# The state product in strips of 32 columns directly behind the output product, and the output product in turns over four column groups

## The chip, the cores and the metric

The kernel runs on one NeuronCore of a Trainium2 chip. The metric is the device time of one execution in microseconds (us), the median of several runs. One further execution was profiled; its trace is what the rows below come from. Engines are named as in the profile: PE (matrix products), PEld (the loading of PE's stationary operand), DVE (vector engine), ACT (scalar engine), POOL, SP (which here issues the DMA transfers).

## The reference

A gated linear recurrence over 768 time steps, for 4 batches and 8 heads of size 48, followed by two pairs of dense layers on the 3072 tokens:

```python
mag = np.sqrt(a_re * a_re + a_im * a_im)
scale = np.minimum(mag, 0.999) / (mag + 1e-06)
...
for t in range(S):
    new_re = ar * S_re - ai * S_im
    new_im = ar * S_im + ai * S_re
    S_re, S_im = (new_re + outer(k[t], v[t]), new_im)
    y[:, :, t] = np.einsum('bhd,bhde->bhe', q[:, :, t], S_re)
x = y as (3072, 384)
h = x @ w_in;   x = (h - tanh(h)) @ w_out       # d_ff 2048
h = x @ w_in2;  r = max(h, 0);  out = (r * r) @ w_out2
```

## The kernel before

**Attention in chunks.** The 768 steps are cut into 6 chunks of 128. One chunk of one batch is a *unit*; there are 24, numbered 4 x chunk + batch. Inside a chunk the recurrence is turned into products: keys and queries are scaled by cumulated decay and phase (`kn`, `qn`; the phase gives each head 96 rows, real and imaginary parts in turns), transposed on PE (`pk`, `pq`, copied by ACT to `kqT`), multiplied to scores (`sc`), masked by DVE (`wm`), and two products follow:

- the *output product* `px` (function `a12`): the masked scores with the values `v` (called intra below), and from chunk 1 on the queries with the state of that batch (inter). Heads of 48 columns are cut into 12 groups G of 32 output columns, so that each product is a 32-column strip which goes to the partitions of column group G % 4 of a PSUM tile, in the k-slice G // 4. A group that holds the seam of two heads has two parts.
- the *state product* `pU` (function `a13`): `kn` with `v` for each of 8 heads, 48 moving columns; DVE then updates the state from it (`a13v`, two instructions). It isn't needed in the last chunk. From chunk 2 on `kn` lies *packed*: heads 0 to 5 as 96 adjacent columns, heads 6 and 7 as three strips of 32 each.

All these are float32, and each such product of the program shows as two MATMUL records in the trace (32 products of a `px` are 64 records). The products of the dense layers are in a split form with single records.

**What runs beside it.** The dense layers are cut into *blocks*: one block is a slice of 128 of d_ff for a group of 512 tokens, 9 products into `h` (L228), ACT and DVE work on `h` (for the first layer pair `t` by tanh, `t<-h,t`, the cast `gh`, the rest `gl`), and, two blocks later, 9 products into `acc` (L260 to L262). A token group is one chunk of all four batches, so chunk c's attention is computed while the blocks of chunk c - 1 run. Chunk 0 runs before all blocks in an order written out by hand (START, up to about 56 us); chunk 1 beside the first 17 blocks, in which DVE also converts the weights (`cv`, `wh`, `wl`) just ahead of their use.

**Order.** A unit has 16 or so steps; its list gives (step, kind, function), units of a chunk start 4 steps apart, and from chunk 2 on each block runs one step of every live unit. Kind "p" stands in front of the block's `h` products, "e", "v", "p2", "v2" behind them. The transposes of `kn` and `qn` are step 13, the scores 14, the output product 15. The state product is in step 15 for chunks 0 to 2 and in step 16, one block later, from chunk 3 on:

```python
(14, "p2" if packed else "p", a11), ..., (15, "p", a12), (15, "v", a12v),
(NST - (c < 3), "p", a13), (NST - (c < 3), "v", a13v),      # NST = 16
```

A scheduler behind the kernel takes this order and its dependences and writes each engine's final row of instructions; each engine works its own row in order. Unit n + 1 makes `kn` and `qn` (DVE, `a9`, behind two ACT sines into `fg`) in the block after unit n's step 15, and its transposes come one block later. The load of `ri` for a later unit is issued by SP in the same stretch, and ACT squares it on arrival (`ab<-ri`, L384).

Of the kernel before, what the change touches and what calls it, by code (L numbers as in the profile page):

```python
# [43 lines left out]
def kernel(  # L44
# [9 lines left out]
    nc = tc.nc  # L54
# [3 lines left out]
    P = 128  # L58
# [4 lines left out]
    KD = DM // P  # L63
    NU = B * NC
    D2 = 2 * D
    HH = H // 2
# [258 lines left out]
    def strip(z, h, i):  # L325
        o = DP * h + 32 * i - (DP - D) * (h % 2)
        return z.rearrange("p h x -> p (h x)")[:, o:o + 32]
# [5 lines left out]
    def unit(n):  # L333
        c, b = divmod(n, B)
        alt = n in (1, 3)
        early_unit = 1 <= n <= 3
        def bank(name):
            if n >= 2:
                return ps_a.tile([P, TG], F32, tag="a", name=name)
            spin[0] = (spin[0] + 1) % 8  # L340
            pool, tag = [(ps_a, "a"), (ps_c, "c"), (ps_h, "h")][(0, 1, 2, 0, 1, 2, 0, 1)[spin[0]]]
            return pool.tile([P, TG], F32, tag=tag, name=name)
# [3 lines left out]
        V = {}  # L346
# [21 lines left out]
        packed = c >= 2  # L368
# [173 lines left out]
        def head(name, h):  # L542
            i, j = slot(h)
            return T(name, i)[:D2, j, :]
# [50 lines left out]
        def a12():  # L595
            px = bank("px")
            vv = V["v"]
            parts = {}
            for G in range(3 * HH):
                r, g = divmod(G, 3)  # L600
                parts[G] = [((2 * r, 0),), ((2 * r, 1), (2 * r + 1, 0)), ((2 * r + 1, 1),)][g]
            for kk in range(KD):
                Gs = range(4 * kk, 4 * kk + 4)
                seq = []
                for inter in ((True, False) if c > 0 else (False,)):
                    for i in range(2):
                        seq += [(G, inter) + parts[G][i] for G in Gs if i < len(parts[G])]
                for j, (G, inter, h, sl) in enumerate(seq):
                    i, jj = divmod(h, HH)
                    if inter:  # L610
                        z, mv = stt[b][:D2], head("qT", h)
                    else:
                        z, mv = vv, V["wm", i][:, jj, :]
                    q0 = 32 * (G % 4)
                    nc.tensor.matmul(  # L615
                        px[q0:q0 + 32, kk * P:(kk + 1) * P],
                        strip(z, h, sl), mv,
                        start=all(e[0] != G for e in seq[:j]),
                        stop=all(e[0] != G for e in seq[j + 1:]),
                    )  # L620
            V["px"] = px

# [15 lines left out]
        def a13():  # L638
            if c + 1 == NC:
                return  # L640
            pU = bank("pU")
            for h in range(H):
                vh = V["v"][:, h, :D]
                hs = slice(h * D, (h + 1) * D)
                if packed and h >= 6:
                    for j in range(3):
                        o = (3 * (h - 6) + j) * P + D2
                        nc.tensor.matmul(
                            pU[32 * j:32 * j + 32, hs], V["kn"][:, o:o + 32], vh,
                            start=True, stop=True,  # L650
                        )
                else:
                    o = h * (P if packed else D2)
                    nc.tensor.matmul(  # L654
                        pU[:D2, hs], V["kn"][:, o:o + D2], vh, start=True, stop=True
                    )
            V["pU"] = pU

# [14 lines left out]
        if c == 0:  # L673
            return dict(
                ld=a0, sq=a1, ln=a2, ph=a3, pc=a6l, ee=a7x, at=a4, pu=a6, rd=a7, lq=l2, lv=l3,
                qe=a8x, sn=a8, er=a7r, kn=lambda: a9((("kn", "k"),)), qn=lambda: a9((("qn", "q"),)),
                t0=t0, e0=t0v, t1=t1_, e1=t1v, s0=lambda: a11((0,)), s1=lambda: a11((1,)),
                m0=lambda: a11v((0,)), m1=lambda: a11v((1,)),
                px=a12, x=a12v, pU=a13, st=a13v, ff=fill,
            )  # L680
# [4 lines left out]
            (12, "e", a8), (12, "e", l3), (12, "e", a9),  # L685
            (13, "p", t0), (13, "v", t0v), (13, "p2", t1_), (13, "v2", t1v),
            (14, "p2" if packed else "p", a11), (14, "v2" if packed else "v", a11v), (15, "p", a12), (15, "v", a12v),
            (NST - (c < 3), "p", a13), (NST - (c < 3), "v", a13v),
        ]

    NST = 16
    plan = {}
    for n in range(B, NU):
        c, b = divmod(n, B)
        s0 = (c - 1) * NM + 3 + 4 * b - (NST - 1)
        for i, kind, f in unit(n):
            plan.setdefault((s0 + int(i), kind), []).append(f)
# [190 lines left out]
    hs, gs = {}, {}  # L888
# [84 lines left out]


    first = {f"{n}{k}": f for n in range(B) for k, f in unit(n).items()}
    first.update(C=clear_pads, W=conv_ahead, J=conv_tick, B=lambda: block_step(0))
    for k in START.split():
# [97 lines left out]
```

## Time and profile before

| | |
|---|---|
| median of 3 runs | 1009.43 us (1008.85 to 1010.75) |
| the profiled execution's own time | 1011.25 us |
| its span, first to last instruction | 1009.3 us |
| PE busy | 983.8 us, 97% of the span |
| ACT busy | 640.0 us, 63% |
| DVE busy | 540.8 us, 54% |

The span is what the trace covers, and the time is the span and some 2 us around it. The shares are means over very unlike stages: attention runs up to about 536 us, the second layer pair alone fills the rest.

### The profile page before, as it was taken

The page shows a single profiled execution, that of the slowest core. Times are in us where ns is not written, and L with a number is a line of the kernel's source. Part 1 is how long each engine was busy: PE and PEld are TensorE (multiplying, and loading weights), DVE is VectorE, ACT ScalarE, POOL GpSimd, SP SyncE. Part 2 cuts the span into 40 slices and gives each one's busy share as a digit, 9 for nine tenths or more (in the row PEclk, how much of TensorE's full clock was granted, in tenths as well). Part 3 has the DMA queues.
Part 4 walks back from the last instruction along what each step waited for, and adds up shares of the span by engine and source line. Part 5 has one row for each costly group of instructions (what it writes and reads, how often), then busy time and mean ns, then how long its engine had stood idle before and what let it go on. Part 6 is the DMA issues. An engine that isn't in the chain of part 4 may idle for free.

```text
span 1009.3 us, 15932 instructions
## 1 busy us (share of the span) xinstructions
PE 983.8 (97%) x6112; PEld 814.5 (81%) x6112; DVE 540.8 (54%) x900; ACT 640.0 (63%) x1132; POOL 17.1 (2%) x37
## 2 busy tenths in 40 slices
PE   3999999999999999999999999999999999999997
PEld 1877788888788888888887888888888888888886
DVE  6899998988866566666534553122232322322111
ACT  8679898766777776667633445456565665555542
POOL 1000000000000000000000000000000000000000
PEclk9999999999999999999999999999999999999999
DMA  7444554665652222112105332025263444330000
GB/s 260 122 126 141 169 147 128 192 192 195 218 144 50 52 82 60 52 51 81 40 23 194 104 95 94 1 79 172 94 207 104 143 140 142 109 110 32 32 0 34
DMA packets 61546, 111.35 MB, mean 110 GB/s; under 512 B 23685, under 2 KB 33177, under 8 KB 61465
## 3 DMA queue, kind: packets, MB, share of 16 engines
q1 hardware_dynamic: 61320, 110.15, 34.9%
q8 instruction: 49, 0.80, 0.3%
q14 instruction: 33, 0.26, 0.1%
q10 hardware_dynamic: 144, 0.13, 0.0%
HBM read 91.29 MB, written 15.76 MB: 106 GB/s over the span
## 4 chain that ended last, share of the span: by engine, by line
PE 80%; DVE 7%; ACT 6%; DMA 5%; issue 1%; SPq 0%; POOL 0%; ACTq 0%; DVEq 0%
PE h L228 33%; PE acc L260 11%; PE acc L262 11%; PE acc L261 11%; PE px L615 4%; PE sc L578 3%; PE pU L654 2%; DMA st<-in_w_dram 2%; ACT L118 2%; DMA ri<-in_ri_dram 2%; PE pq L553 1%; PE pk L553 1%; ACT ab L125 1%; DVE cv L161 1%; DVE gl L249 1%
## 5 line engine op out<-in xcount | busy, mean ns | idle before, releaser
L249 DVE TENSOR_TENSOR gl<-t,gh 128x512 fp32r<-128x512 f32 (+1 forms) x193 | 132.4, 686 | 251.9 <-ACT gh L248 251.6
L228 PE MATMUL h<-xh,wh 128*128 128x512 f32 (+1 forms) x579 | 230.8, 399 | 0.3 <-DVE t L244 0.3
L260 PE MATMUL acc<-gh,wh 128*128 128x512 f32 (+1 forms) x579 | 227.7, 394 | 1.5 <-ACT x2t L271 1.4
L228 PE MATMUL h<-xl,wh 128*128 128x512 f32 (+1 forms) x579 | 225.8, 390 | 0.0
L228 PE MATMUL h<-xh,wl 128*128 128x512 f32 (+1 forms) x579 | 225.4, 389 | 0.0
L262 PE MATMUL acc<-gh,wl 128*128 128x512 f32 (+1 forms) x579 | 225.3, 389 | 0.0
L261 PE MATMUL acc<-gl,wh 128*128 128x512 f32 (+1 forms) x579 | 225.2, 389 | 0.0
L248 ACT CAST gh<-t 128x512 fp32r<-128x512 f32 (+1 forms) x193 | 118.9, 617 | 71.5 <-PE acc L262 63.5
L246 ACT ACTIVATE t<-h 128x512 f32<-128x512 f32 x96 | 57.4, 598 | 126.2 <-PE h L228 126.2
L228 PEld LDWEIGHTS h<-xh,wh 128*128 128x128 f32 x579 | 108.7, 188 | 26.2 <-issue 2.6
L260 PEld LDWEIGHTS acc<-gh,wh 128*128 128x128 f32 x579 | 108.8, 188 | 23.4 <-ACT x2t L271 2.6
L228 PEld LDWEIGHTS h<-xh,wl 128*128 128x128 f32 x579 | 108.7, 188 | 23.2
L262 PEld LDWEIGHTS acc<-gh,wl 128*128 128x128 f32 x579 | 108.7, 188 | 22.9
L228 PEld LDWEIGHTS h<-xl,wh 128*128 128x128 f32 x579 | 108.8, 188 | 21.0 <-DVE xl L634 0.2
L261 PEld LDWEIGHTS acc<-gl,wh 128*128 128x128 f32 x579 | 108.8, 188 | 20.8
L125 ACT ACTIVATE t<-h 128x512 f32<-128x512 f32 (+1 forms) x97 | 57.2, 590 | 66.9 <-PE h L228 65.3
L118 ACT ACT_TABLE_LOAD x66 | 84.7, 1283 | 2.0 <-PEq L1057 0.8
L244 DVE TENSOR_TENSOR t<-h,t 128x512 f32<-128x512 f32 (+1 forms) x97 | 65.9, 680 | 35.9 <-ACT t L125 35.7
L247 ACT ACTIVATE t<-t 128x512 f32<-128x512 f32 x96 | 60.3, 628 | 1.6
L192 DVE TENSOR_TENSOR wmin<-wmin,cz 128x768 bf16<-128x768 bf16 x32 | 17.8, 557 | 57.4 <-ACT cz L189 57.4
L578 PEld LDWEIGHTS sc<-kqT 96*128 96x128 f32 x352 | 42.7, 192 | 2.0 <-ACT kqT L562 0.2
L578 PE MATMUL sc<-kqT 96*128 96x128 f32 x352 | 43.5, 276 | 0.0
(128 smaller groups left out, 1078.1 us busy)
## 6 DMA issues: line engine op xcount, KB each, us to landing
st<-in_w_dram SPq DMA_DIRECT2D x32, 768.0 KB, 4.6
sr<-in_w_dram SPq DMA_DIRECT2D x32, 768.0 KB, 4.7
ri<-in_ri_dram SPq DMA_DIRECT2D x24, 384.0 KB, 4.1
qk<-in_qk_dram SPq DMA_DIRECT2D x24, 384.0 KB, 5.6
w2d<-cv SPq DMA_DIRECT2D x16, 384.0 KB, 2.6
jw<-w2d SPq DMA_DIRECT2D x16, 384.0 KB, 3.0
vz<-in_v_dram SPq DMA_DIRECT2D x21, 256.0 KB, 3.1
x2d<-x2t SPq DMA_DIRECT2D x18, 256.0 KB, 2.4
```

The lines of the kernel that those rows point to most:

```text
L118: load = nc.scalar.preload_act_table_set(name).ins
L125: r = nc.scalar.activation(*a, **kw)
L228: nc.tensor.matmul(h, w_[:, kk * P:(kk + 1) * P], x_[:, kk, cs], start=(i == 0), stop=(i == n - 1),)
L244: nc.vector.tensor_tensor(t, h, t, op=ALU.subtract)
L246: last["act"] = nc.scalar.activation(t, h, AF.Relu).ins
L247: nc.scalar.activation(t, t, AF.Square)
L248: nc.scalar.copy(gh, t)
L249: nc.vector.tensor_tensor(gl, t, gh.bitcast(F32), op=ALU.subtract)
L260: nc.tensor.matmul(o, wh[:, sl], gh, start=first, stop=False)
L261: nc.tensor.matmul(o, wh[:, sl], gl, start=False, stop=False)
L262: nc.tensor.matmul(o, wl[:, sl], gh, start=False, stop=end)
L578: nc.tensor.matmul(sc[:, j, :], head("kT", i * HH + j), head("qT", i * HH + j), start=True, stop=True,)
```

## The change

Three edits. (1) In `a12` the 32 products of a unit (16 in chunk 0) are no longer issued slice by slice; each of the four column groups gets its own list (groups g, g + 4, g + 8, each with its inter and intra parts), and the lists are issued in turns, one product of each column group after the other. (2) In `a13` every head, not only the two packed apart, is cut into three strips of 32 stationary columns: 24 products in place of 8 (chunks 0 and 1) or 12 (chunks 2 to 4). (3) From chunk 3 on the state product and the state update move from step 16 to step 15, as it is in the chunks before.

```diff
+            lists = [
+                [
+                    (G, inter) + part
+                    for G in range(g, 3 * HH, 4)
+                    for inter in ((True, False) if c > 0 else (False,))
+                    for part in parts[G]
+                ]
+                for g in range(4)
+            ]
-            for kk in range(KD):
-                Gs = range(4 * kk, 4 * kk + 4)
-                seq = []
-                for inter in ((True, False) if c > 0 else (False,)):
-                    for i in range(2):
-                        seq += [(G, inter) + parts[G][i] for G in Gs if i < len(parts[G])]
-                for j, (G, inter, h, sl) in enumerate(seq):
+            for k in range(len(lists[0])):
+                for g, seq in enumerate(lists):
+                    G, inter, h, sl = seq[k]
...
                 hs = slice(h * D, (h + 1) * D)
-                if packed and h >= 6:
-                    for j in range(3):
+                for j in range(3):
+                    if packed and h >= 6:
                         o = (3 * (h - 6) + j) * P + D2
-                        nc.tensor.matmul(
-                            pU[32 * j:32 * j + 32, hs], V["kn"][:, o:o + 32], vh,
-                            start=True, stop=True,
-                        )
-                else:
-                    o = h * (P if packed else D2)
+                    else:
+                        o = h * (P if packed else D2) + 32 * j
                     nc.tensor.matmul(
-                        pU[:D2, hs], V["kn"][:, o:o + D2], vh, start=True, stop=True
+                        pU[32 * j:32 * j + 32, hs], V["kn"][:, o:o + 32], vh,
+                        start=True, stop=True,
                     )
...
-            (NST - (c < 3), "p", a13), (NST - (c < 3), "v", a13v),
+            (NST - 1, "p", a13), (NST - 1, "v", a13v),
```

**PE, unit 13 (chunk 3, batch 1).** The state product before stands alone between the `acc` products of one block and the `h` products of the next; the output product (`px`, state of batch 1) stands 19 rows ahead of it, before nine `h` and nine `acc` products:

```order
L260 MATMUL acc<-gh,wh_5_767 128x512
L261 MATMUL acc<-gl,wh_5_767 128x512
L262 MATMUL acc<-gh,wl_5_768 128x512
L654 MATMUL pU<-vz,kn_3146 96x48 x6
L648 MATMUL pU<-vz,kn_3146 32x48 x6
L228 MATMUL h<-xh_2068,wh_8_953 128x512
L228 MATMUL h<-xl_2069,wh_8_953 128x512
```

In the changed kernel it follows the last strips of the same unit's output product (`wm_13_3471` and `wm_13_3473` are the masked scores of the two head halves, `kqT` the transposed queries):

```order
L622 MATMUL px<-kqT_147,state_142 32x128
L622 MATMUL px<-kqT_146,state_142 32x128
L622 MATMUL px<-wm_13_3473,vz 32x128
L622 MATMUL px<-kqT_147,state_142 32x128
L622 MATMUL px<-wm_13_3473,vz 32x128 x4
L657 MATMUL pU<-vz,kn_3336 32x48 x24
L228 MATMUL h<-xh_2208,wh_7_962 128x512
```

The 96-column products are gone, 24 strips stand in one piece, and the block's `h` products follow them at once. The order of the `h` and `acc` products among themselves is the same from chunk 2 on.

**DVE, the same unit.** Before, the first half of the state update stands behind `gl` and right ahead of the next unit's `kn`, the second half behind `qn`:

```order
L634 TENSOR_TENSOR xl_3098<-px,xh_3097 128x3x128
L385 SCALAR_TENSOR_TENSOR ab_3462,chk_m<-ab_3462 128x384
L244 TENSOR_TENSOR t<-h,t 128x512
L249 TENSOR_TENSOR gl<-t,gh 128x512
L666 TENSOR_TENSOR state_142<-state_142,pU 96x8x48
L524 TENSOR_TENSOR kn_3404<-qk_3006,fg_3165 128x6x96
L530 TENSOR_TENSOR kn_3404<-qk_3006,fg_3165 128x6x32
L524 TENSOR_TENSOR qn_3407<-qk_3006,fg_3165 128x6x96
L530 TENSOR_TENSOR qn_3407<-qk_3006,fg_3165 128x6x32
L667 TENSOR_TENSOR state_142<-state_142,rall 96x8x48
```

In the changed kernel both halves stand behind `xl`, ahead of `ab`:

```order
L641 TENSOR_TENSOR xl_3299<-px,xh_3298 128x3x128
L670 TENSOR_TENSOR state_142<-state_142,pU 96x8x48
L671 TENSOR_TENSOR state_142<-state_142,rall 96x8x48
L385 SCALAR_TENSOR_TENSOR ab_3662,chk_m<-ab_3662 128x384
L244 TENSOR_TENSOR t<-h,t 128x512
L249 TENSOR_TENSOR gl<-t,gh 128x512
L524 TENSOR_TENSOR kn_3606<-qk_3182,fg_3353 128x6x96
```

Nothing that waits for `pU` is left between `gl` and `kn`.

**ACT, behind the output product of unit 9 (chunk 2, batch 1).** The scheduler also moves a few instructions of ACT, DVE and SP that the edits don't name. Before, `ab<-ri` (the square of a load that has to arrive) stands ahead of the block's `t`:

```order
L633 ACTIVATE xh_2068,chk_y<-px 128x3x128
L384 ACTIVATE ab_2419<-ri_2373 128x768
L125 ACTIVATE t<-h 128x512
L118 ACT_TABLE_LOAD
L125 ACTIVATE fg_2121<-fg_2121 128x384
L248 CAST gh<-t 128x512
L125 ACTIVATE fg_2121<-fg_2121,b_hpi 128x384
```

In the changed kernel:

```order
L640 ACTIVATE xh_2208,chk_y<-px 128x3x128
L125 ACTIVATE t<-h 128x512
L118 ACT_TABLE_LOAD
L125 ACTIVATE fg_2261<-fg_2261 128x384
L248 CAST gh<-t 128x512
L125 ACTIVATE fg_2261<-fg_2261,b_hpi 128x384
L384 ACTIVATE ab_2571<-ri_2525 128x768
```

In unit 9 the square has moved behind both sines. In units 12 and 16 the reverse happens: before, it stands behind the sines, now ahead of `t`. In the other units from 10 to 18 it stands ahead of `t` in both kernels, in unit 8 behind the sines in both.

## Rows read from the trace of the kernel before

**Rows 1.** The profile's page: busy time; the chain that ended last, by engine.

```profile
PE 983.8 (97%) x6112; PEld 814.5 (81%) x6112; DVE 540.8 (54%) x900; ACT 640.0 (63%) x1132; POOL 17.1 (2%) x37
...
PE 80%; DVE 7%; ACT 6%; DMA 5%; issue 1%; SPq 0%; POOL 0%; ACTq 0%; DVEq 0%
```

**Rows 2.** Windows by stage, busy us of each engine: chunks 1, 2 and 4.

```profile
core 0: us, PE busy (x) PEld busy (x) DVE busy (x) ACT busy (x) POOL busy (x), PEclk, DMA share, GB/s
...
56.00:163.00 107.00, 105.36 (x783) 85.73 (x783) 102.78 (x172) 96.90 (x162) 0.00 (x0) 1.00 0.47 140
163.00:272.80 109.80, 109.14 (x835) 91.54 (x833) 93.65 (x162) 79.88 (x144) 0.00 (x0) 1.00 0.62 199
...
369.60:466.40 96.80, 96.80 (x772) 81.83 (x771) 59.49 (x110) 68.46 (x123) 0.00 (x0) 1.00 0.22 61
```

**Rows 3.** Windows of tile px alone (PE, PEld, DVE, ACT): units of chunks 0 and 2.

```profile
42.70:44.20 1.50, 1.10 (x32) 0.84 (x32) 0.00 (x0) 0.04 (x1) 1.00 0.65 102
...
174.00:177.50 3.50, 2.25 (x64) 1.98 (x64) 0.00 (x0) 0.42 (x2) 1.00 0.73 257
```

**Rows 4.** Groups of PE by shape, whole span (busy us, mean ns).

```profile
L615 PE MATMUL px<-wm,vz 128*32 128x128 f32 x672 | 41.2, 274 | 0.0
...
L654 PE MATMUL pU<-vz,kn 128*96 128x48 f32 x224 | 21.8, 248 | 0.0
...
L648 PE MATMUL pU<-vz,kn 128*32 128x48 f32 x144 | 4.5, 212 | 0.0
```

**Rows 5.** Timeline of PE, chunk 1 (start us, length us).

```profile
101.69 1.56 PE L654 MATMUL pU<-vz,kn 128*96 128x48 f32 x16
103.07 0.48 PE L228 MATMUL h<-xh,wh 128*128 128x512 f32 x1
```

**Rows 6.** Timeline of PE, unit 8 of chunk 2.

```profile
174.80 0.32 PE L615 MATMUL px<-kqT,state 96*32 96x128 f32 x4
...
176.97 1.22 PE L654 MATMUL pU<-vz,kn 128*96 128x48 f32 x12
178.12 0.37 PE L648 MATMUL pU<-vz,kn 128*32 128x48 f32 x12
178.42 0.50 PE L228 MATMUL h<-xh,wh 128*128 128x512 f32 x1
178.76 0.39 PE L228 MATMUL h<-xl,wh 128*128 128x512 f32 x1
```

**Rows 7.** Timeline of PE, the state product of unit 14 (chunk 3).

```profile
327.65 1.14 PE L654 MATMUL pU<-vz,kn 128*96 128x48 f32 x12
328.72 0.37 PE L648 MATMUL pU<-vz,kn 128*32 128x48 f32 x12
329.02 0.50 PE L228 MATMUL h<-xh,wh 128*128 128x512 f32 x1
```

**Rows 8.** Chain that ended last, in START.

```profile
54.92 1.49 PE pU L654 x16
```

**Rows 9.** Timeline of ACT behind the output products of units 8 and 10.

```profile
180.81 0.60 ACT L125 ACTIVATE t<-h 128x512 f32<-128x512 f32 x1 [3.15 <-PE h L228]
...
229.74 0.85 ACT L384 ACTIVATE ab<-ri 128x768 f32<-128x768 f32 x1 [3.71 <-DMA ri<-in_ri_dram]
```

**Rows 10.** Timeline of DVE: qn behind unit 10; gl and qn behind unit 14.

```profile
235.67 0.35 DVE L530 TENSOR_TENSOR qn<-qk,fg 128x192 f32<-128x192 f32 x1
...
329.62 0.68 DVE L249 TENSOR_TENSOR gl<-t,gh 128x512 fp32r<-128x512 f32 x1
...
331.83 0.35 DVE L530 TENSOR_TENSOR qn<-qk,fg 128x192 f32<-128x192 f32 x1
```

**Rows 11.** Timeline of PE: transposes behind unit 10; acc and transposes behind unit 14.

```profile
236.17 0.52 PE L553 MATMUL pq<-ident,qn 128*128 128x128 f32 x3 [0.17 <-DVE qn L530]
...
331.58 0.39 PE L260 MATMUL acc<-gh,wh 128*128 128x512 f32 x1
331.81 0.40 PE L261 MATMUL acc<-gl,wh 128*128 128x512 f32 x1
...
333.98 0.38 PE L553 MATMUL pq<-ident,qn 128*128 128x128 f32 x2
```

More of the change, by code (lines that the diff above doesn't have):

```diff
@@ L613, in a12 @@
                         z, mv = vv, V["wm", i][:, jj, :]
-                    q0 = 32 * (G % 4)
+                    kk = G // 4
                     nc.tensor.matmul(
-                        px[q0:q0 + 32, kk * P:(kk + 1) * P],
+                        px[32 * g:32 * g + 32, kk * P:(kk + 1) * P],
                         strip(z, h, sl), mv,
-                        start=all(e[0] != G for e in seq[:j]),
-                        stop=all(e[0] != G for e in seq[j + 1:]),
+                        start=k == 0 or seq[k - 1][0] != G,
+                        stop=k + 1 == len(seq) or seq[k + 1][0] != G,
                     )
```

## Prediction

> **What bounds the kernel now.** I read the page first: PE is busy for 97% of the span and carries 80% of the chain that ended last [rows 1]. A mean hides stages, so the windows by stage come next. In chunks 2 and 4 PE is busy nearly all of the time, DVE 85% and 61% of it. In chunk 1 it is close: PE 105.4 of 107 us, DVE 102.8, ACT 96.9 [rows 2]. So PE time that is saved in chunks 3 to 5 should shorten the run, and in chunk 1 most of it should turn into a wait for DVE, which converts weights just ahead of their use. Then the timeline of PE shows what the two products cost, and the timelines of ACT and DVE how late the work arrives on which PE waits next.
>
> **The output product in turns.** Records of one kind overlap: each lasts 0.27 us [rows 4], but a unit's 64 cover 2.25 us, so their starts stand (2.25 - 0.27) / 63 = 31 ns apart; the 32 of chunk 0, which has no inter parts, stand (1.10 - 0.27) / 31 = 27 ns apart [rows 3]. In full turns I take 27 ns for all: 63 x 0.0268 = 1.69 us from the first start to the last, where it is 1.98. The gain is 0.29 a unit (bounds: 0, since each column group has 16 records in either order, and 0.29, since no row shows these shapes at a faster pace), in the 20 units from chunk 1 on, none in chunk 0. The masked scores are wanted one product earlier than before, which costs nothing: the scores are step 14, a block ahead of `px`.
>
> **The state product in strips.** A 96-column record costs (1.22 - 0.25) / 11 = 88 ns; the 12 records of strips that follow in the same unit stand (0.37 - 0.21) / 11 = 15 ns apart [rows 4, 6]. A head is two records of the former or six of the latter, 176 against 89 ns. New: 47 x 0.0149 = 0.70 us from first to last start, and 0.14 to the next full-width start, as now (178.42 - 178.12 less 11 x 0.015) [rows 6]. Only 12 records in a row were ever seen at this pace, and 48 are asked for. The bounds are 15 ns and the 27 ns of `px`.
> [...]
>
> **Directly behind.** From `px`'s last start to the first 96-column start is now 176.97 - 174.80 - 1.98 = 0.19 us [rows 3, 6]. Both products are 32-column strips after the change; I take 0.10, halfway between nothing and 0.19. In chunks 3 and 4 the state product stands alone: it costs 329.02 - 327.65 = 1.37 us [rows 7], and the first `h` behind strips takes 178.76 - 178.42 = 0.34 where full-width records stand 0.23 apart [rows 6, 11]. That 0.11 is paid once and no longer twice.
>
> **The sum on PE**, from `px`'s first start to the next `h`. After, for all units with both products: 1.69 + 0.10 + 0.70 + 0.14 = 2.63.
> Chunk 1: 2.17 + 1.38 = 3.55 [rows 5, 6], gain 0.92, four units, 3.7.
> Chunk 2: 178.42 - 174.80 = 3.62, gain 0.99, 4.0.
> Chunks 3 and 4: 2.17 + 1.37 + 0.11 = 3.65, gain 1.02, eight units, 8.2.
> Chunk 5: `px` alone, 4 x 0.29 = 1.2.
> START: four state products of 1.38 at 0.84, 2.2.
> PE is freed of 19.3 us in all.
>
> **What of it arrives.** START: PE is the chain there [rows 8], so I credit nearly all, 2.0. Chunk 1: DVE has 107 - 102.8 = 4.2 us to give in the whole stage [rows 2], some of which no order can fill. Of 3.7 I credit 1.2 (bounds 0 and 3.7).
> Chunks 2 to 4 hang on a chain of unit n's block: the load of `ri` lands, ACT squares it, then `t`, the sines, `gh`; DVE makes `gl`, `kn`, `qn`; PE transposes. Where the square stands ahead of `t`, ACT stood still for 3.71 us until the load came [rows 9], an instant that a faster PE does not move. Behind unit 10 `qn` ends at 236.02 and PE waited for it [rows 10, 11]; a PE that comes 0.99 earlier waits 0.99 longer. So in units 10 and 11 I credit 0.1 together. In units 8 and 9 the square now stands behind the sines, and ACT waits for `h` itself [rows 9], which moves with PE: full, 2.0. From chunk 3 on the same chain has room: `qn` ends at 332.18 and PE wants it at 333.98, 1.80 later; `gl` ends at 330.30 and is wanted at 331.81, 1.51 later [rows 10, 11]. Both exceed the 1.02 by which PE comes earlier, and the state update between `gl` and `kn` goes away. Units 12 and 16 newly get the square ahead of `t`, and unit 12 still has weight conversions on DVE: I take off 0.4. Chunks 3 and 4 give 7.8, chunk 5 its 1.2. The update moved into step 15 is hidden behind ACT's wait for `ri`; without that cover its two instructions put DVE about 1 us later, within the 1.5.
> Sum: 2.0 + 1.2 + 2.1 + 7.8 + 1.2 = 14.3 us. The profiled execution took 1011.25, so 997.0; it stood 1.8 above the median of the runs, which gives 1009.4 - 14.3 = **995.1 us**.
>
> **The rivals.**
> *All of PE's gain arrives*: DVE's lag in chunk 1 and ACT's wait in units 10 and 11 turn out to have slack after all. 1009.4 - 19.3 = 990.1. For it: PE's own waits in these stages are short (0.17 in rows 11). Against it: the 4.2 us above.
> *The turns bring nothing*, the balance between column groups having been enough: 0.29 less in some 15 credited units, 4.5, so 999.6. Chunk 0's 27 ns speaks against it.
> *A floor per record*: strips that keep on for 48 records go at `px`'s 27 ns. 47 x 0.0268 = 1.26 in place of 0.70, 0.56 lost in each: START 0, chunk 1 0.5, chunk 2 1.0, chunks 3 and 4 3.5, chunk 5 1.2, which gains 6.2: 1003.2.
> [...]
> *The feeders bind further*: in chunks 3 and 4 half is lost to `gl` and `qn` (3.9), START and chunk 1 give nothing (3.2): 1002.2. For it: the room there is only 0.5 more than the gain.
> *Slower*: strips in a long row don't overlap and each record costs what a 96-column one does, 88 ns. 48 of them take 47 x 0.088 + 0.14 = 4.3; a unit takes 6.1 where it took 3.6, 2.5 lost in 16 units and 2.9 in each of four of START, less 1.2 of chunk 5: some 50 us, 1060. It decides at the pace where a unit breaks even, (3.62 - 1.69 - 0.10 - 0.14) / 47 = 36 ns a record. Against it: both strips seen, 15 and 31 ns, are below.
>
> **Chances and range.** The forecast 0.50 (its own range 992.5 to 998.5: chunk 1 from 0 to 3, the 0.10 either way, 0.4 of unit 12), all arrives 0.20, turns bring nothing 0.10, feeders 0.11, floor 0.05, slower 0.04. From the best case with no pause between the two products (16 x 0.1 below 990.1: 988.5) to the feeders' case, 1002.5. This leaves out the slower case, the floor and the edges. 0.2% of the time, 2 us, is about what a measurement of this kernel can tell from no change: faster 0.93, same 0.03, slower 0.04.
>
> **What will show it.** A unit's `px` covering 1.96 us in place of 2.25; `pU` x48 covering some 0.9 us; 2.6 us from `px` to `h` in chunks 2 to 4; units of chunk 4 at 23.2 us from one to the next where they were 96.8 / 4 = 24.2 [rows 2]; longer waits of `pq` for `qn` in units 10 and 11; in chunk 1 more PE idle time for DVE with DVE at 98% or more. The prediction is wrong if 48 strips stand over 20 ns apart, or if chunks 3 and 4 show waits of PE for `gl` or `qn`.

## The result, and the profile after

The changed kernel took 1002.04 us in the median of 5 runs (999.33 to 1003.11), beside 1009.43 for the kernel before; the ratio is 0.9914 (95% interval 0.9895 to 0.9934), so it is faster by 0.9%. Run once more, beside some of the experiments (e8 below), it stood at 0.9896 (0.9877 to 0.9914). The experiments ran on four chips, on which the kernel before took 1011.5 to 1012.9 us, so they are compared by their ratio to it on the same chip; 0.001 is about 1 us. The profiled execution took 1001.31 us where that of before took 1011.25.

The page of the changed kernel (span, busy time, chain that ended last) answers to [rows 1]:

```profile
span 999.3 us, 17016 instructions
...
PE 963.5 (96%) x6656; PEld 796.5 (80%) x6656; DVE 541.1 (54%) x900; ACT 639.6 (64%) x1132; POOL 17.1 (2%) x37
...
PE 73%; ACT 10%; DMA 7%; DVE 7%; issue 2%; SPq 1%; POOL 0%; ACTq 0%; DVEq 0%; POOLq 0%
```

PE has 20.3 us less to do, and the span is only 10.0 us shorter. PE's share of the chain fell from 80 to 73%; ACT, DMA and DVE took it over. The windows by stage (chunks 1, 2, 3, 4; columns as in [rows 2]) say where:

```profile
53.50:159.00 105.50, 101.51 (x926) 81.74 (x916) 102.77 (x172) 96.70 (x165) 0.00 (x0) 1.00 0.48 142
159.00:270.60 111.60, 105.99 (x932) 88.46 (x930) 96.40 (x166) 80.11 (x144) 0.00 (x0) 1.00 0.65 207
270.60:364.70 94.10, 92.74 (x869) 78.52 (x869) 61.86 (x113) 68.11 (x122) 0.00 (x0) 1.00 0.29 79
364.70:457.80 93.10, 92.68 (x865) 78.45 (x864) 59.61 (x110) 68.21 (x123) 0.00 (x0) 1.00 0.23 64
```

PE now stands still for 4.0 us in chunk 1, 5.6 in chunk 2, and 1.4 and 0.4 in chunks 3 and 4. Before it stood for 1.6 in chunk 1 and 0.7 in chunk 2.

What PE's work costs came out as forecast. Windows of `px` alone and PE's groups by shape, then PE's timeline in unit 14 of the changed kernel (answering to [rows 3], [rows 4], [rows 7]):

```profile
317.50:321.50 4.00, 1.97 (x64) 1.70 (x64) 0.34 (x1) 0.58 (x2) 1.00 0.21 30
```

```profile
L622 PE MATMUL px<-wm,vz 128*32 128x128 f32 x672 | 35.8, 273 | 0.0
...
L657 PE MATMUL pU<-vz,kn 128*32 128x48 f32 x816 | 15.0, 206 | 0.0
```

```profile
318.51 0.43 PE L622 MATMUL px<-kqT,state 96*32 96x128 f32 x8
...
320.07 0.40 PE L622 MATMUL px<-wm,vz 128*32 128x128 f32 x8
320.29 0.85 PE L657 MATMUL pU<-vz,kn 128*32 128x48 f32 x48
321.08 0.50 PE L228 MATMUL h<-xh,wh 128*128 128x512 f32 x1
```

`px` covers 1.97 us. The 48 strips start (0.85 - 0.21) / 47 = 13.6 ns apart, and stand 0.09 us behind the last start of `px` (320.07 + 0.40 - 0.27 = 320.20). From `px` to `h` it is 321.08 - 318.51 = 2.57 us.

The waits show what went wrong. PE's timeline behind units 10 and 12:

```profile
230.54 0.52 PE L553 MATMUL pk<-ident,kn 128*128 128x128 f32 x3 [1.48 <-DVE kn L530]
231.48 0.52 PE L553 MATMUL pq<-ident,qn 128*128 128x128 f32 x3 [0.42 <-DVE qn L530]
```

```profile
283.00 0.52 PE L553 MATMUL pk<-ident,kn 128*128 128x128 f32 x3 [0.94 <-DVE kn L530]
283.93 0.52 PE L553 MATMUL pq<-ident,qn 128*128 128x128 f32 x3 [0.42 <-DVE qn L530]
```

In the first of these passes PE waits once more, at the scores, for the transfers that lay out `kqT`. SP's timeline shows them in two pieces. Between the pieces stands the store of a converted weight, which waited 1.9 us for DVE (in the kernel before, all six transfers went out in one piece and PE didn't wait):

```profile
241.58 0.46 PE L578 MATMUL sc<-kqT 96*128 96x128 f32 x2 [0.84 <-DMA kqT<-kqT]
```

```profile
233.90 1.99 SPq L568 DMA_DIRECT2D kqT<-kqT  x3
237.82 0.33 SPq L171 DMA_DIRECT2D w2d<-cv  x1
238.25 1.88 SPq L568 DMA_DIRECT2D kqT<-kqT  x3
```

The table gives the time from one unit's first `px` start to the next's (from PE's timelines; e8 is a second profiled execution of the changed kernel; the others are the runs below: e1 turns alone, e2 strips alone, e3 no move, e4 late square, e6 later conversions, e7 three buffers, e10 both cuts).

| units | before | after | e8 | e1 | e2 | e3 | e4 | e6 | e7 | e10 |
|---|---|---|---|---|---|---|---|---|---|---|
| 8 to 9 | 24.14 | 23.05 | 23.63 | 23.96 | 23.94 | 23.12 | 23.56 | 24.39 | 23.95 | 23.08 |
| 9 to 10 | 24.23 | 23.07 | 23.06 | 25.20 | 23.39 | 23.06 | 23.07 | 23.60 | 23.42 | 23.08 |
| 10 to 11 | 24.50 | 26.65 | 26.89 | 23.96 | 28.02 | 26.60 | 24.06 | 23.08 | 25.38 | 23.08 |
| 11 to 12 | 25.17 | 26.60 | 25.87 | 25.92 | 25.45 | 26.12 | 25.94 | 23.08 | 23.63 | 23.08 |
| 12 to 13 | 24.24 | 24.80 | 24.67 | 23.91 | 23.75 | 23.43 | 23.08 | 24.50 | 23.08 | 23.08 |
| 13 to 14 | 24.18 | 23.08 | 23.08 | 23.95 | 23.71 | 23.47 | 23.08 | 23.08 | 23.08 | 23.08 |
| 16 to 17 | 24.18 | 23.74 | 24.19 | 23.95 | 23.71 | 23.47 | 23.08 | 23.08 | 23.08 | 23.08 |

Where nothing holds PE up a unit takes 23.08 us, 1.11 less than before. From unit 10 to 11 and from 11 to 12 it takes 2.15 and 1.43 more than before. The two executions of the changed kernel differ by up to 0.7 us for a unit of chunk 2, so smaller differences there say nothing.

**The theory.** Behind a unit's last `qn` there is a closed loop of latencies. Its pieces on DVE, SP and ACT of the changed kernel, from the `qn` behind unit 10 to that behind unit 11:

```profile
230.98 0.35 DVE L530 TENSOR_TENSOR qn<-qk,fg 128x192 f32<-128x192 f32 x1
...
235.97 0.96 DVE L505 TENSOR_TENSOR qk<-qk,ee 128x768 f32<-128x768 f32 x1 [1.00 <-DMA qk<-in_qk_dram]
...
245.88 0.54 DVE L428 SCALAR_TENSOR_TENSOR tl<-ri,th 128x384 fp32r<-128x384 f32 x1
...
257.58 0.35 DVE L530 TENSOR_TENSOR qn<-qk,fg 128x192 f32<-128x192 f32 x1
```

```profile
231.36 0.33 SPq L487 DMA_DIRECT2D qk<-in_qk_dram  x1
...
247.82 0.35 SPq L377 DMA_DIRECT2D ri<-in_ri_dram  x1
```

```profile
251.66 0.85 ACT L384 ACTIVATE ab<-ri 128x768 f32<-128x768 f32 x1 [5.01 <-DMA ri<-in_ri_dram]
252.41 0.58 ACT L125 ACTIVATE t<-h 128x512 f32<-128x512 f32 x1
```

`qn` ends at 231.33 and frees the one buffer of `qk`; SP issues its load at once; DVE has other rows first, until 234.97, and then stands still for the last 1.00 us until the load lands. The product of `qk` frees the buffer of `ee`. Then come the exponentials into it, logarithms and arctan on ACT, `tl` on DVE, which frees the buffer of `ri`; its load; the square, behind which `t`, the sines, `kn` and `qn` stand. From `qn` to `qn` that is 257.93 - 231.33 = 26.60 us, with next to nothing of PE in it. From the start of the square to the end of `qn` it takes 6.27 us, all of it behind the load; where the square stands behind the sines (e4 below), `t`, the sines, `kn` and `qn` need not wait for that load. In the kernel before, the last `qn` ended at 211.52, 236.02 [rows 10] and 260.84 behind units 9, 10 and 11: 24.50 and 24.82 apart, little more than PE's 24.2 us. The rivals: DVE and the DMA queue are simply full of layer-1 weight conversions in chunk 2, whatever the order; the move of the state product did the damage; or the turns bring nothing.

### The profile page after: what moved, and what is told of

It reads as the page before. It is cut to its first block, busy times and chain, and to the rows that moved or that the text cites. A ratio compares the mean times of both kernels' runs of the same rounds, so it can differ in the third digit from the quotient of the medians.

```text
span 999.3 us, 17016 instructions
## 1 busy us (share of the span) xinstructions
PE 963.5 (96%) x6656; PEld 796.5 (80%) x6656; DVE 541.1 (54%) x900; ACT 639.6 (64%) x1132; POOL 17.1 (2%) x37
## 4 chain that ended last, share of the span: by engine, by line
PE 73%; ACT 10%; DMA 7%; DVE 7%; issue 2%; SPq 1%; POOL 0%; ACTq 0%; DVEq 0%; POOLq 0%
PE h L228 32%; PE acc L260 11%; PE acc L262 11%; PE acc L261 11%; PE px L622 3%; ACT L118 2%; DMA ri<-in_ri_dram 2%; PE sc L578 2%; DMA qk<-in_qk_dram 2%; ACT ab L125 2%; DMA st<-in_w_dram 2%; PE pq L553 1%; ACT ee L125 1%; ACT ri L125 1%; PE pk L553 1%
## 5 line engine op out<-in xcount | busy, mean ns | idle before, releaser
L260 PEld LDWEIGHTS acc<-gh,wh 128*128 128x128 f32 x579 | 108.8, 188 | 23.2 <-ACT x2t L271 2.7
```

The costliest lines, as they stand in the source:

```text
L260: nc.tensor.matmul(o, wh[:, sl], gh, start=first, stop=False)
```

## Experiments

**Turns alone** (e1: the new `a12` in the kernel before) and **strips alone** (e2: the new `a13` there, at the old steps).

> The kernel before with the output product in turns alone; the state product stays in 96-column records and at its old step. Theory (PE's prices are as forecast, and what was lost of the gain was lost to a chain of ACT, DVE and two loads behind units 10, 11, 12 and 16): a unit's px covers about 1.96 us in place of 2.25, chunks 3 and 4 gain 8 x 0.28 = 2.2, chunk 5 1.1, chunk 1 and chunk 2 about 1 together, so 4 to 5 us in all, 1004.5 to 1005.5. Rival (the turns bring nothing, all of the gain is the strips'): 1009.4, px still 2.25.

> The kernel before with the state product in strips alone, at its old step; the output product in its old order. Theory: START gains 2.4, chunk 1 about 1, chunks 3 and 4 8 x 0.6 = 4.8, chunk 2 loses 1 to 2 by the chain behind units 10 and 11, where the order of DVE's conversions follows the strips: 7 in all, 1002 to 1003.5. Rival (the strips alone bring the whole 7.4 and the turns nothing): 1002.0 as well, so this run tells the two apart only together with the turns alone. Rival (a second loss that comes only with both edits): 998 to 1000, chunk 2 then gains.

Turns alone: 0.9959 (0.9941 to 0.9978), 4.1 us, so they do bring something. `px` covers the 1.97 us again, the next record starts 0.28 earlier, and 0.24 a unit is left of it in chunks 3 and 4, since the `h` behind it take some 0.04 longer. Strips alone: 0.9918 (0.9900 to 0.9935), 8.2 us. I expected about 7, which is within the interval. In chunks 3 and 4 a unit gains 0.48. PE's timeline of e2 in unit 14, where the state product stands alone: 48 strips take 0.81 to the next `h`, where it was 1.37 [rows 7]:

```profile
325.40 0.88 PE L650 MATMUL pU<-vz,kn 128*32 128x48 f32 x48
326.21 0.50 PE L228 MATMUL h<-xh,wh 128*128 128x512 f32 x1
```

Unit 10 takes 3.5 us longer than before with the strips alone already (28.02), so the loss in chunk 2 needs neither the turns nor the move.

**No move** (e3: all but edit 3).

```diff
-            (NST - 1, "p", a13), (NST - 1, "v", a13v),
+            (NST - (c < 3), "p", a13), (NST - (c < 3), "v", a13v),
```

> The changed kernel with one part undone: the state product of chunks 3 and 4 goes back to one step behind the output product. Behind units 12 and 16 the square of ri then stands behind the sines again. Theory: units 12 and 16 give back some 1.7 and 0.7 us, the first h behind the strips is paid for twice again in eight units (0.9 us): 1000 to 1001.5. Rival (the order of the square is harmless, only PE's charge counts): slower than the changed kernel, 1002.5 to 1003.

0.9883 (0.9865 to 0.9901), 11.8 us; the changed kernel has 0.9896, so the move brings nothing that can be measured here. The table shows two halves that cancel. Without it units 12 and 16 lose nothing (the square stands behind the sines there), and every unit of chunks 3 and 4 takes 23.47 in place of 23.08. The move is worth 0.39 a unit where it doesn't call up the loop, 3.1 us in eight units, where I had put 0.9 for paying the first `h` twice. That it did the damage falls: chunk 2 loses the same without it.

**The square of `ri` behind the second sine** (e4 in the changed kernel; e5, the same edge in the kernel before).

```diff
+                if n - 3 in sines:
+                    es.enter_context(tc.issue_after(sines[n - 3]))
                 nc.scalar.activation(t, V["ri"], AF.Square)
...
-            lut(V["cs"][:, HD:], G, AF.Sin, scale=-TWO_PI, bias=b_hpi)
+            sines[n] = lut(V["cs"][:, HD:], G, AF.Sin, scale=-TWO_PI, bias=b_hpi).ins
```

> The changed kernel, with the square of ri issued behind the second sine of the block in every unit from 9 on, by an order edge and with no other edit. Theory (behind units 10 to 12 and 16 ACT stands still for the load of ri ahead of t, and PE then waits for kn and qn): units 10 to 12 and 16 take 23.1 us instead of 26.7, 26.6, 24.8 and 23.7, so 6 to 8 us less, 994 to 996, and no wait of pk for kn over 0.5 us in chunks 2 to 4. Rival (DVE and the DMA queue are full of layer-1 conversions in chunk 2, the place of the square does not matter): 1000.5 to 1002, with the waits of pk for kn still there.

> Control: the same order edge (square of ri behind the second sine) in the kernel before. Theory (with PE at 24.2 us a unit the chain of ACT, DVE and two loads has just room, only behind units 10 and 11 it has none): 0.3 to 1.5 us less than before, so 0.9985 to 0.9997 of it; the change's own gain between this kernel and the changed one with the same edge is then 15 us. Rival (the late square is an improvement of its own that has nothing to do with the change): 5 us or more less than before, 0.995 or lower.

e4: 0.9836 (0.9816 to 0.9857), 6 us less than the changed kernel. e5: 0.9993 (0.9982 to 1.0004), no gain that can be told from none. So the late square is worth something only where PE is fast. ACT's timeline of e4 behind unit 10, where `t` now waits for PE and the square for nothing:

```profile
223.59 0.60 ACT L125 ACTIVATE t<-h 128x512 f32<-128x512 f32 x1 [1.59 <-PE h L228]
...
227.05 0.61 ACT L125 ACTIVATE fg<-fg,b_hpi 128x384 f32<-128x384 f32 x1
227.57 0.83 ACT L388 ACTIVATE ab<-ri 128x768 f32<-128x768 f32 x1
```

From unit 12 on each interval is 23.08. In chunk 2 not all is back: PE's timeline of e4 shows the masked scores late, behind a conversion on DVE:

```profile
243.95 0.30 PE L626 MATMUL px<-wm,vz 128*32 128x128 f32 x1 [1.81 <-DVE wm L594]
```

**Later conversions** (e6 in the changed kernel; e9 in the kernel before): one third of a layer-1 conversion in each block from the 38th on (about the start of chunk 3), held behind a `gl` of that block on DVE.

```diff
-        nc.vector.tensor_tensor(gl, t, gh.bitcast(F32), op=ALU.subtract)
+        glast[0] = nc.vector.tensor_tensor(gl, t, gh.bitcast(F32), op=ALU.subtract).ins
...
-        if (t >= NATT - 14 or (t >= NB0 + 4 and t % 3 == 0)) and cdone[0] < len(cq):
-            conv_tick()
+        if t >= NB0 + 20 and cdone[0] < len(cq):
+            with tc.issue_after(glast[0]):
+                conv_tick()
```

> The changed kernel with the layer-1 weight conversions (DVE work, 768 KB loads, 384 KB stores) taken out of chunk 2 and done one third of a conversion in each block of chunks 3 to 5; the square of ri stays where the scheduler puts it, ahead of t behind units 8 to 15. Theory (it is the length of a loop qn, load of qk, product, exp, log, arctan, load of ri, square, t, sines, kn, qn, and any cut brings it under PE's 23.1 us): units 10 to 12 take 23.1 to 23.6 us, 994 to 997.5 on the scale of 1009.4 before, 0.985 to 0.988. Rival (the place of the square alone makes the loss, whatever DVE and the queue carry): units 8 to 11 all lose now, 1002 or more, 0.9925 or higher.

> Control for the run with later conversions: the same move of the layer-1 conversions out of chunk 2, in the kernel before. Theory (at PE's 24.2 us a unit the loop had room without it, but for units 10 and 11): 0 to 2.5 us less than before, 0.9975 to 1.000, so the change's own gain on this footing is 16 to 18 us. Rival (the later conversions are worth some 8 us by themselves): 0.993 or lower.

e6: 0.982 (0.9808 to 0.9833), 7.7 us less than the changed kernel. The scheduler now puts the square ahead of `t` behind all units from 8 to 15, and units 10, 11 and 13 to 15 still take 23.08: an early square alone makes no loss, which speaks for the loop and against the square's place as a cause by itself. It isn't quite clean, since units 8, 9 and 12 take 24.39, 23.60 and 24.50: the passes from `qn` to `qn` behind units 7, 8 and 11 are still too long, 24.45, 23.59 and 25.40 us. e9: 0.9984 (0.9972 to 0.9997), 1.6 us.

**A third buffer for `ri`** (e7), another cut of the same loop, and the changed kernel beside it (e8).

```diff
-            t = pair("ri", "re", "im", pool=ap2)
+            t = pair("ri", "re", "im", pool=ap2, bufs=3)
```

> The changed kernel with three buffers for ri in place of two and no other edit: the load need not wait for tl of the unit before the last, and lands about a block earlier; the square then stands ahead of the copy of px, with its data there. Theory: ACT's wait for the load behind units 10 to 12 and 16 goes from 3.3 to 5.0 us to under 0.5, pk's wait for kn with it; 994 to 996.5, 0.985 to 0.987. Rival (the DMA queue is too full in chunk 2 to bring it earlier): ACT still waits for ri by 2 us or more, 1000 to 1002.

> The changed kernel itself, on the chip of the runs beside it: 0.9914 of before (0.9895 to 0.9934), with the waits of pk for kn behind units 10 to 12. Both theories expect the same; it is the mark for the other three, and for the one with the state product left a step later (0.9883).

e7: 0.9847 (0.9835 to 0.9860), 5 us less than the changed kernel, with nothing but a buffer added. ACT's timeline of e7: the square runs ahead of the copy of `px`, with no wait in front of it, so the queue did bring the load earlier:

```profile
220.72 0.84 ACT L384 ACTIVATE ab<-ri 128x768 f32<-128x768 f32 x1
221.46 0.47 ACT L640 ACTIVATE xh<-px 128x384 fp32r<-128x384 f32 x1
...
222.98 0.60 ACT L125 ACTIVATE t<-h 128x512 f32<-128x512 f32 x1 [0.95 <-PE h L228]
```

ACT waits for `ri` no more in chunks 2 and 3, as expected, and from unit 12 on each interval is 23.08. In chunk 2 not all is back: unit 10 takes 25.38, and the longest wait of PE there is again for `kqT` (PE's timeline of e7):

```profile
240.97 0.46 PE L578 MATMUL sc<-kqT 96*128 96x128 f32 x2 [1.38 <-DMA kqT<-kqT]
```

e4 and e7 leave the conversions where they were and still bring 5 to 6 us, so the rival of a DVE and a queue that are simply full, whatever the order, doesn't hold. That the conversions have a part in the loss is shown by e6, and by the masked scores of e4.

**Both cuts** (e10: later conversions and late square; e11: later conversions and three buffers; e12: later conversions and late square in the kernel before).

> The changed kernel with both cuts: later layer-1 conversions and the square of ri behind the second sine. Theory (one cut brings the loop under PE's 23.1 us, a second one finds little left): chunks 3 and 4 as with one cut, 1.1 us a unit over before; in chunk 2 up to 2 us more than with later conversions alone: 0.980 to 0.9825. Rival (the two losses add up): 6 us more than with later conversions alone, 0.976.

> The changed kernel with later layer-1 conversions and three buffers for ri. Theory: as with both cuts above, 0.980 to 0.9825, PE's waits over 0.4 us in chunks 2 to 4 gone except those for kn and qn behind unit 8. Rival (the losses add up): 0.976.

> The kernel before with both cuts (later layer-1 conversions, square of ri behind the second sine), as the mark for the changed kernel with both, 0.9777. Theory (the old PE time of 24.2 us a unit hides the chain nearly everywhere): 0.9975 to 0.999, so that the three edits are worth 19.5 to 21.5 us where the feeders are out of the way, beside 19.3 us of PE time freed by the sum. Rival (half of what the two cuts bring has nothing to do with the edits): 0.989 to 0.992, and the edits are worth 12 to 14 us.

e10: 0.9777 (0.9760 to 0.9795), 989.13 us; e11: 0.9769 (0.9751 to 0.9787), 988.54 us, the fastest kernels here. My expectation was too small: the second cut finds 4 to 5 us more, close to the rival's 0.976. The table says why: one cut leaves other units late (e4 units 10 and 11, by DVE and the masked scores; e6 units 8, 9 and 12, by the square; e7 unit 10). Windows of e10, chunks 2 to 4: PE never stands still, and DVE has 70 of 110 us in chunk 2:

```profile
160.00:270.00 110.00, 110.00 (x1055) 93.68 (x1054) 70.33 (x131) 83.32 (x150) 0.00 (x0) 1.00 0.25 71
270.00:363.00 93.00, 93.00 (x869) 79.14 (x868) 70.28 (x127) 69.05 (x124) 0.00 (x0) 1.00 0.42 127
363.00:456.00 93.00, 93.00 (x824) 78.92 (x823) 70.51 (x126) 68.73 (x123) 0.00 (x0) 1.00 0.39 123
```

e12: 0.9978 (0.9964 to 0.9991), 2.2 us. So 0.9777 / 0.9978 = 0.980: with the feeders out of the way the three edits are worth 20 us (18 to 22 by the two intervals), as the 19.3 us of freed PE time in the sum had it.

## Why the prediction was right or wrong

The sign held and the prices on PE held. The result is just inside the range, and that is luck: the upper end, 1002.5, was set by a rival that put the loss elsewhere, and the forecast's own range of 992.5 to 998.5 was missed. Of the gain, 14.3 us were forecast; 7.4 came between the medians and 10.0 between the two profiled executions. Credited and measured, by the lead of the one execution's `px` starts over the other's:

| | credited | measured |
|---|---|---|
| START | 2.0 | 2.5 |
| chunk 1 | 1.2 | 1.0 |
| units 8 and 9 | 2.0 | 2.3 |
| units 10 and 11 | 0.1 | -3.6 |
| units 12 and 16 | 1.6 | -0.1 |
| the six others of chunks 3 and 4 | 6.1 | 6.5 |
| chunk 5 to the end | 1.2 | 1.4 |

**The turns** were priced at 0.29 and gave 0.28 to the next start, 0.24 net. The rival in which they bring nothing falls by e1.

**The strips** were priced at 15 ns; 48 in a row keep 13.6. The floor per record falls, and so does the slower case, far from its 36 ns.

**Directly behind**: the pause was taken as 0.10 and is 0.09. PE's gain in chunks 3 and 4 is 1.11 a unit and not 1.02. By parts it is 0.24 of the turns, 0.48 of the strips and 0.39 of the move, where the sum had 0.29, 0.53 and 0.20 (0.09 of pause and 0.11 of `h`). Of the move's other 0.19, 0.09 is a pause that the sum left out: strips start 0.32 us behind an `acc` product (325.08 and 325.40 in e2), and full-width records stand 0.23 apart. The last 0.1 is open.

**Chunk 1**: DVE is busy 102.77 of 105.50 us there, 97% and not the 98 I named; the 1.0 us is what it left.

**The step that failed** is "an instant that a faster PE does not move [...] a PE that comes 0.99 earlier waits 0.99 longer. So in units 10 and 11 I credit 0.1 together". I took the landing of `ri` for a fixed instant. It is the end of a loop that starts at the last `qn`, and the loop got longer: 26.08 and 26.60 us behind units 9 and 10 where it had been 24.50 and 24.82, so PE lost not its gain alone but 3.6 us more. The pass behind unit 10, cut into pieces (from the timelines of DVE, SP and ACT), shows where:

| piece of the pass | before | after | e6 |
|---|---|---|---|
| end of `qn` to the product of `qk` | 3.24 | 4.64 | 3.14 |
| to the end of `tl` | 10.41 | 10.45 | 10.45 |
| to SP's issue of the load of `ri` | 0.25 | 1.40 | 0.02 |
| to the square | 4.65 | 3.84 | 2.97 |
| to the end of the next `qn` | 6.27 | 6.27 | 6.28 |
| sum | 24.82 | 26.60 | 22.86 |

So 1.40 us came with the load of `qk`, and 1.15 because SP issued the load of `ri` later, behind transfers of `rall` that kept it until 247.39; 0.81 came back, since that load was then quicker. With the conversions moved away (e6) the pass is shorter than PE's 23.08. In the kernel before, DVE made the product of `qk` at 239.26, 3.21 after SP had issued the load at 236.05, without a wait (timelines of DVE and SP of the kernel before):

```profile
211.17 0.35 DVE L530 TENSOR_TENSOR qn<-qk,fg 128x192 f32<-128x192 f32 x1
...
239.26 0.96 DVE L505 TENSOR_TENSOR qk<-qk,ee 128x768 f32<-128x768 f32 x1
...
249.12 0.55 DVE L428 SCALAR_TENSOR_TENSOR tl<-ri,th 128x384 fp32r<-128x384 f32 x1
...
260.49 0.35 DVE L530 TENSOR_TENSOR qn<-qk,fg 128x192 f32<-128x192 f32 x1
```

```profile
236.05 0.33 SPq L487 DMA_DIRECT2D qk<-in_qk_dram  x1
...
249.92 0.77 SPq L377 DMA_DIRECT2D ri<-in_ri_dram  x1
```

In the changed kernel it came 4.61 after the issue (235.97 and 231.36 above). A pass earlier, DVE had waited 1.30 us for the weights of a conversion, which the scheduler had put ahead of that product (DVE's timeline of the changed kernel; the product came 6.8 us after the `qn` that ended at 205.25, where before it had come 3.2 after):

```profile
204.90 0.34 DVE L530 TENSOR_TENSOR qn<-qk,fg 128x192 f32<-128x192 f32 x1
...
208.09 0.56 DVE L157 TENSOR_SCALAR cv<-st 128x768 int32<-128x768 int32 x1 [1.30 <-DMA st<-in_w_dram]
...
212.10 0.96 DVE L505 TENSOR_TENSOR qk<-qk,ee 128x768 f32<-128x768 f32 x1
```

What made the load of `qk` slower is not settled: in the 6 to 7 us ahead of its issue the DMA engines were 94 to 97% busy in both kernels, and with the conversions away the product still came 3.0 to 4.4 us after the issue (e10), where PE didn't have to wait for it. Nor does any run change DVE's row order alone, so how much of the 3.6 us is owed to the order and how much to the faster PE is open. What is shown is that three different cuts of the loop each bring 5 to 8 us in the changed kernel, and the two of them that were tried in the kernel before 0 to 2 there.

**Units 12 and 16**: "I take off 0.4" was the right mechanism (the square moves ahead of `t`) with too small a size: the two lost 2.2 us (1.02 + 0.56 and 1.02 - 0.44), and e3 and e4 give it back. The sign by which the prediction said it would be wrong, waits of PE for DVE in chunk 3, is there behind unit 12 (0.94 and 0.42 us). Of the other six units five take 23.08 us, where 23.2 was forecast, and unit 19 takes 23.25.

**The feeders bind further** was the rival whose time, 1002.2, came nearest. It had the loss in START, chunk 1 and throughout chunks 3 and 4; the loss lies in chunk 2 and in two units behind it. **All of PE's gain arrives** was a rival at 990.1. It is what the edits do once the loop is cut (e10, e11).

## What to carry to other kernels

When a bottleneck engine gets faster, look for loops of latencies that don't pass through it: a buffer freed by the last reader, the load that waits for it, and the work on other engines that makes the next last reader. Follow one from an event to the same event a unit later, and compare its length with the new period and not with the old; to say that a wait stays where it is, is a claim on such a loop. Here ACT stood in front of a load for 5.01 us and so held up `t`, the sines, `kn` and `qn` behind it; a third buffer or an order edge then brought 5 and 6 us more, where the change itself had brought 7.4 (e7, e4).

## What was unexpected of the hardware

Float32 strips of 32 stationary columns, in turns over three column groups with 48 moving columns, start 13.6 ns apart over 48 records in a row, about half of the 27 ns of `px` (four groups, 128 moving columns). A load of 384 KB (`qk`) for which DVE stood waiting reached it between 3.0 us (e10, issued at 226.37 for a product at 229.39) and 7.1 us (e4, issued at 229.77 for a product at 236.87) after its issue on the same queue; in the changed kernel behind unit 10, 1.4 us of it went straight into the loop. ACT stood still for 5.01 us in front of the square, and `t` and the first sine, which stand behind it, started at 252.41 and 254.30; in e4, where the square stands behind the sines, ACT waited 1.59 us for PE ahead of `t`, and not for the load.
